# Channel weights from two loads instead of six, first items' channel products moved up, and extra TensorE products between the last weight groups

## The chip, the cores and the metric

The kernel runs on one core of a Trainium2 chip. The metric is device time in microseconds (us) of one execution. Three runs of the kernel before took 184.38, 184.82 and 185.29 us; the median is 184.82.

The core has TensorE (PE in the profile; its weight loads, which overlap products, are PEld), VectorE (DVE), ScalarE (ACT), GpSimd (POOL) and SyncE (SP). [...]

## The reference

A causal convolution with softmaxed taps per head, then a spectral mix of 64 modes, then a channel product with a residual:

```python
def _attn_ref(x, weight):                     # x: 8 x 3264 x 192, weight: 8 x 7
    w = exp(weight - max) / (sum + 1e-09)     # per head, 7 taps
    ...
    out = np.einsum('hk,bskhg->bshg', w, x_unf)

def _moe_ref(x, w_r, w_i, w_ch):              # x is the convolution's result
    X = np.fft.rfft(x, axis=1)
    Xr, Xi = (np.real(X[:, :n_modes]), np.imag(X[:, :n_modes]))
    Yr = np.einsum('bmd,mde->bme', Xr, w_r) - np.einsum('bmd,mde->bme', Xi, w_i)
    Yi = np.einsum('bmd,mde->bme', Xr, w_i) + np.einsum('bmd,mde->bme', Xi, w_r)
    Y[:, :n_modes] = Yr + 1j * Yi
    y = np.fft.irfft(Y, n=S, axis=1)
    u = x + y
    return u + np.maximum(u @ w_ch, 0.0)
```

## The kernel before

Instructions stand in the order in which the program emits them on each engine (a manual schedule); only the waits are added.

**Loads.** x comes in 13 units (`load_unit`, line 136), two transfers each, issued by POOL; units 6 to 12 are issued at lines 240 and 241. Then come six loads of the channel weights `w_ch` (192 x 192): rows 0 to 127 into `wm`, rows 128 to 191 into partitions 64 to 127 of `w1`, rows 128 to 191 into both halves of `wt2`, and rows 64 to 127 and 0 to 63 into the two halves of `wsw`. The right halves of `wm` and `w1` hold an identity. Then come the mode weights, 16 groups of four modes, two transfers of 288 KB each (`load_w`, line 250): eight groups in a row, and each further group when a mix has freed its place. Eight POOL transfers are in flight at most: each issue waits for the one eight places before it.

**Convolution and forward transform.** `conv_pass` multiplies x by band matrices and writes the result back into `xall`, one slot further left (x of the first unit is loaded from slot 1 on, its result starts in slot 0). `dft` multiplies it by a table of cosines and sines; `xtrans` transposes the sums.

**Mix.** The main loop runs over pairs of groups, d = 0 to 7. `mix(g, bank)` (line 400) makes twelve products of 192 columns from the transposed spectrum and the group's weights; `mix_copy` (ACT) takes the result out of PSUM, `mix_trans` transposes it, DVE and ACT copy it into `yet`. In between, `some(n)` takes jobs off the list `tjobs`: `g_bank` and `c_bank`, which transpose the table and the convolved x, eight tiles each, into `ftab` and `ct`. The bank pairs are `zm` (mix) and `ze` (its transposes); four more (`zt4`) serve the jobs.

**The seam.** After the last pair, `zw_mm(b, bank)` multiplies `yet` by `wm` and `w1`, 384 columns each, for the eight batches b; the left 192 columns are the product with the channel weights ("g"), the right 192 the spectrum itself ("y"). `zw_out` copies both, scaled, into `zw`, by DVE or ACT. These eight share the four banks of `zm` and `ze`, so b = 4 to 7 wait for the copies of b = 0 to 3. Items 0 and 1 of the output (`place[0]`, `place[1]`) are done here one product at a time: `c_products(n)` (channel product of the convolved x, six products for each of two halves), `full(n, "g", a)` (adds the spectral share of the channel product), a relu, `full(n, "y", a)` (adds y), and `finish(n)` (DVE adds the convolved x, SP stores).

**The loop.** From line 568 on the other 50 items follow with the same parts (`both`, `relu` on ACT, `finish`) on four bank pairs, two of them laid over the banks of `zm` and `ze`, the first over that of b = 4 and 5.

`wt2` and `wsw` are the right-hand sides for the second and third column block of a "c" product, lines 439 and 440.

Of the kernel before, what the change touches and what calls it, by code (L numbers as in the profile page):

```python
# [9 lines left out]
ALU = mybir.AluOpType  # L10
ACT = mybir.ActivationFunctionType
AX = mybir.AxisListType
F32 = mybir.dt.float32
BF16 = mybir.dt.bfloat16
# [5 lines left out]
def kernel(  # L20
# [9 lines left out]
    nc = tc.nc  # L30
    B, S, D = x.shape
# [5 lines left out]
    P = 128  # L37
# [4 lines left out]
    NT = 2 * NB  # L42
# [8 lines left out]
    units = [(q, b0, n) for q in range(NQ) for b0, n in (UNITS if q else UNITS0)]  # L51
# [3 lines left out]
    def sb(name, shape, dtype):  # L55
        return pool.tile([P] + shape, dtype, tag=name, name=name)
# [5 lines left out]
    xall = sb("xall", [NSLOT, 2, D], BF16)  # L62
# [5 lines left out]
    zw = mixa[:, 0:2 * B * D].rearrange("p (t b d) -> p t b d", t=2, b=B)  # L68
    band = sb("band", [H, 2 * P], BF16)
    wm = sb("wm", [2 * D], BF16)  # L70
    w1 = sb("w1", [2 * D], BF16)
    wt2 = sb("wt2", [D], BF16)
    wsw = sb("wsw", [D], BF16)
    ident = sb("ident", [P], BF16)
    perm = sb("perm", [P], BF16)
    ascale = sb("ascale", [1], F32)
# [40 lines left out]
    def open_psum(side, widths):  # L117

        if side in stacks:
            stacks.pop(side).close()  # L120
        es = ExitStack()
        n = npool[0]
        npool[0] += 1
        p = es.enter_context(tc.tile_pool(name=f"ps{n}", bufs=1, space=PSUM, side=side, reuse_waits="tile"))
        stacks[side] = es
        return [p.tile([P, w, 512], F32, tag=f"z{n}_{i}", name=f"z{n}_{i}") for i, w in enumerate(widths)]
# [9 lines left out]
    def load_unit(q, b0, n):  # L136
        t0 = 2 * b0
        nf = min(2 * n, NF - t0)
        s0 = NT * q + t0 + 1
        for i in range(2):  # L140
            off = ((2 * q + i) * S + P * t0) * D
            src = bass.AP(tensor=x.tensor, offset=x.offset + off, ap=[[D, P], [P * D, nf], [1, D]])
            nc.gpsimd.dma_start(out=xall[:, s0:s0 + nf, i, :], in_=src)  # L143
# [24 lines left out]
    for _ in range(NIDLE):  # L168
        nc.tensor.matmul(ZC[2][:, 0, 0:2 * D], xall[:, 0, 0, 0:P], xall[:, 0, :, :], start=True, stop=True,
                         skip_group_check=True)  # L170
    nc.vector.tensor_scalar(out=cidx[:, 0:PW], in0=cidx[:, 0:PW], scalar1=goff[:, 0:1], scalar2=None, op0=ALU.add)
    for k in range(KK):
        nc.vector.tensor_scalar(out=masks[:, PW * k:PW * (k + 1)], in0=cidx[:, 0:PW],
                                scalar1=float(KK - 1 - k), scalar2=None, op0=ALU.is_equal)
# [16 lines left out]
    for g in range(4):  # L191
        dst, srcv = band[32 * g:32 * g + 32, :, 32 * g:32 * g + PW], pk3[32 * g:32 * g + 32, :, :]
# [39 lines left out]
    for u in units[4:6]:  # L232
# [4 lines left out]
                            fill=1.0, base=0, pattern=[[-1, D]], channel_multiplier=1)  # L237
    nc.gpsimd.affine_select(out=w1[64:P, D:2 * D], in_=w1[64:P, D:2 * D], compare_op=ALU.not_equal,
                            fill=1.0, base=P, pattern=[[-1, D]], channel_multiplier=1)
    for u in units[6:]:  # L240
        load_unit(*u)
    nc.gpsimd.dma_start(out=wm[:, 0:D], in_=moe_w_ch[0:P, :])
    nc.gpsimd.dma_start(out=w1[64:P, 0:D], in_=moe_w_ch[P:D, :])
    for i in range(2):
        nc.gpsimd.dma_start(out=wt2[64 * i:64 * i + 64, :], in_=moe_w_ch[P:D, :])
        nc.gpsimd.dma_start(out=wsw[64 * i:64 * i + 64, :], in_=moe_w_ch[64 - 64 * i:P - 64 * i, :])

    NG = MODES // 4

# [104 lines left out]
    zt4 = open_psum("left", (1, 1, 1, 1))  # L354
    z4 = open_psum("right", (1, 1, 1, 1))
    ze, zm = [z[:, 0, :] for z in z4[0:2]], [z[:, 0, :] for z in z4[2:4]]
    for z in zm:
        nc.vector.memset(z[:, 0:2 * D], 0.0)
    tbank = [0]
# [28 lines left out]
            trans(tp[:, P * k:P * k + P], row[:, P * w:P * w + P])  # L388
        copy(ct[:, k0:k0 + 8, :].rearrange("p t s -> p (t s)"), tp[:, 0:8 * P])

    tjobs = [(g_bank, 8 * k, min(8, NT - 8 * k)) for k in range((NT + 7) // 8)]
    tjobs += [(c_bank, k) for k in range(0, 3 * NT * NQ, 8)]

    def some(n):
        for _ in range(n):
            if tjobs:
                f, *a = tjobs.pop(0)
                f(*a)

    def mix(g, bank):  # L400
        yp = bank[:, D * (g % 2):D * (g % 2) + D]
        for j in range(3):
            for p4 in range(4):
                m = 4 * g + p4
                nc.tensor.matmul(yp[32 * p4:32 * p4 + 2 * B, :], xt[:, j, :, m],  # L405
                                 wts[g][:, p4, j, :], start=(j == 0), stop=(j == 2),
                                 tile_position=(0, 32 * p4), skip_group_check=True)
        if g < NW:
            load_w(g + NW + 3)
        elif g >= NW + 3:  # L410
            load_w(g + NW)

    def mix_copy(d, bank, g0, n):
        nc.scalar.copy(out=ymix[d % 2][:, g0:g0 + n, :],  # L414
                       in_=bank[:, D * g0:D * (g0 + n)].rearrange("p (g d) -> p g d", g=n))

    def mix_trans(d, g0, n):
        et = [z.bitcast(BF16)[:, 0:n * P].rearrange("p (g k) -> p g k", g=n) for z in ze]
        for t in range(2):
            for g in range(n):  # L420
                trans(et[t][:, g, :], ymix[d % 2][:, g0 + g, 64 * t:64 * t + P])
        m0 = 8 * d + 4 * g0
        for t in range(2):
            dst = yet[:, t, :, :].rearrange("p b (c m) -> p c b m", c=2)[:, :, :, m0:m0 + 4 * n]
            srcv = et[t].rearrange("p g (q k) -> p (g q) k", q=4)[:, :, 0:16].rearrange(
                "p m (c b) -> p c b m", c=2)
            if t == 0:
                nc.vector.tensor_copy(out=dst, in_=srcv)
            else:
                nc.scalar.copy(out=dst, in_=srcv)  # L430

    def z_pieces(u, row, which):
        r = slice(64 * row, 64 * row + 64)
        q, t = u
        if which == "c":
            b0, b1 = slice(0, D), slice(D, 2 * D)
            lhs = [ct[r, 3 * (NT * q + t) + w, :] for w in range(3)]
            if row == 0:
                return [(b0, lhs[0], wm[r, 0:D]), (b0, lhs[1], wt2[r, :]), (b1, lhs[2], wsw[r, :])]
            return [(b0, lhs[0], wm[r, 0:D]), (b1, lhs[1], wsw[r, :]), (b1, lhs[2], wt2[r, :])]  # L440
        return [(slice(0, 2 * D), ftab[r, t, :],
                 zw[r, 0 if which == "g" else 1, 2 * q:2 * q + 2, :].rearrange("p b d -> p (b d)"))]

# [27 lines left out]
    def zw_mm(b, bank):  # L471
        nc.tensor.matmul(bank[:, 0:2 * D], yet[:, 0, b, :], wm[:], start=True, stop=False)  # L472
        nc.tensor.matmul(bank[:, 0:2 * D], yet[:, 1, b, :], w1[:], start=False, stop=True)  # L473

    def zw_out(b, bank, on_scalar=None):
        dst = zw[:, :, b, :]
        srcv = bank[:, 0:2 * D].rearrange("p (t d) -> p t d", t=2)
        if on_scalar or (on_scalar is None and b % 2):
            nc.scalar.activation(out=dst, in_=srcv, func=ACT.Copy, scale=ascale[:, 0:1])
        else:  # L480
            nc.vector.tensor_scalar(out=dst, in0=srcv, scalar1=ascale[:, 0:1], scalar2=None, op0=ALU.mult)
# [3 lines left out]
    place = {}  # L485
# [22 lines left out]
    def c_products(n):  # L508
        for first in range(2):
            both(n, first, "c", begin=(first == 0))  # L510

    def full(n, which, a):
        (q, t), _ = duos[n]
        nc.tensor.matmul(place[n][0][a][:, 0:2 * D], ftab[:, t + a, :],  # L514
                         zw[:, 0 if which == "g" else 1, 2 * q:2 * q + 2, :].rearrange("p b d -> p (b d)"),
                         start=False, stop=(which == "y"), skip_group_check=True)
# [2 lines left out]
    while pend:  # L519
        xtrans(pend.pop(0), ze)  # L520
    ND = NG // 2
    for d in range(ND - 1):
        mix(2 * d, zm[d % 2])
        mix(2 * d + 1, zm[d % 2])
        mix_copy(d, zm[d % 2], 0, 2)
        some(4 if d < ND - 2 else 2)
        mix_trans(d, 0, 2)
        some(4 if d < ND - 2 else 99)
    sl = open_psum("left", (1, 1, 2))
    place[0] = ([z[:, 0, :] for z in sl[0:2]], None)  # L530
    place[1] = ([sl[2][:, i, :] for i in range(2)], sl[2])
    d = ND - 1
    mix(NG - 2, zm[1])
    mix_copy(d, zm[1], 0, 1)
    c_products(0)
    mix_trans(d, 0, 1)
    c_products(1)
    mix(NG - 1, zm[0])
    mix_copy(d, zm[0], 1, 1)
    mix_trans(d, 1, 1)  # L540
    zb4 = zm + ze
    for b in range(4):
        zw_mm(b, zb4[b])
    for b in range(4):
        zw_out(b, zb4[b])
    for a in range(2):
        full(0, "g", a)
    b0, b1 = place[0][0]
    nc.vector.tensor_scalar(out=b0[:, 0:2 * D], in0=b0[:, 0:2 * D], scalar1=0.0, scalar2=None, op0=ALU.max)
    nc.scalar.activation(out=b1[:, 0:2 * D], in_=b1[:, 0:2 * D], func=ACT.Relu)  # L550
    for b in range(4, 6):
        zw_mm(b, zb4[b - 4])
    for a in range(2):
        full(0, "y", a)
    for a in range(2):
        full(1, "g", a)
    for b in range(4, 6):
        zw_out(b, zb4[b - 4], True)
    finish(0)
    for b in range(6, 8):  # L560
        zw_mm(b, zb4[b - 4])
    relu(1)
    for b in range(6, 8):
        zw_out(b, zb4[b - 4], False)
    zz = open_psum("right", (2, 2))
    zz = [zz[1], None, zz[0], None]

    for n in range(2, N + 2):
        if n == 3:
            zz[1::2] = open_psum("left", (2, 2))  # L570
        if n < N:
            z = zz[(n - 2) % 4]
# [48 lines left out]
```

## Time and profile before

| | |
|---|---|
| median of three runs | 184.82 us |
| profiled execution, its own time | 183.83 us |
| its span in the profile | 182.1 us |
| TensorE busy | 162.3 us (89%) |
| DVE, ACT, POOL busy | 113.7, 98.4, 51.3 us |
| mean granted TensorE clock | 0.968 |
| loaded by POOL's queue (as written) | 19.64 MB |
| stored by SP's queue | 20.09 MB |

The prediction's sums are made against the profiled execution. A row of the timeline has start and duration in us, engine, line, operation, what is written and read, shapes, the count, and in brackets the engine's idle time before it and what ended it. A row of a stretch has from and to, its length, the busy time of PE, PEld, DVE, ACT and POOL with counts, the granted clock (1.00 is full), the busy share of the DMA engines (packets overlap, so it can pass 1) and GB/s. A row of the chain of waits has start, duration and what it was. "idle before" and releasers are inferred from semaphores.

### The profile page before, as it was taken

What the parts mean: (1) busy time and instruction counts of PE and PEld (TensorE: products, weight loads), DVE (VectorE), ACT (ScalarE), POOL (GpSimd) and SP (SyncE); (2) the same over time, 40 slices, a digit from 0 to 9 for tenths busy, and PEclk for the clock granted to TensorE, in tenths of its full rate; (3) what the DMA queues carried; (4) which work ended last, traced back from release to release, by engine and by line L of the source; (5) the groups of instructions that cost most, each with busy time, mean ns of one, the idle gap of its engine ahead of it and who ended that gap; (6) DMA issues with size and microseconds to landing.
All of it is one profiled execution on the core that took longest, in us unless ns stands there. A gap on an engine that the chain in (4) does not pass through costs nothing.

```text
span 182.1 us, 6281 instructions
## 1 busy us (share of the span) xinstructions
PE 162.3 (89%) x2738; PEld 124.2 (68%) x2738; DVE 113.7 (62%) x173; ACT 98.4 (54%) x138; POOL 51.3 (28%) x82
## 2 busy tenths in 40 slices
PE   7978979999999988999774389999999999999980
PEld 3567969999999967988673135566666666666640
DVE  6679864365455446766581005678777877877782
ACT  6348774344434435766643115566666666666650
POOL 7998844443232944444441000000000000000000
PEclk9999999999999999999999756999999999999998
DMA  4999999999999999999999930468988898888886
GB/s 53 148 188 191 193 191 192 193 191 192 193 192 169 172 205 206 208 205 206 208 205 207 206 59 0 158 238 315 336 303 315 320 315 324 311 327 317 316 320 223
DMA packets 50139, 40.12 MB, mean 220 GB/s; under 512 B 28608, under 2 KB 50112, under 8 KB 50112
## 3 DMA queue, kind: packets, MB, share of 16 engines
q0 software_dynamic: 35808, 19.64, 78.6%
q1 hardware_dynamic: 14304, 20.09, 30.1%
q8 instruction: 21, 0.34, 0.8%
q14 instruction: 6, 0.05, 0.1%
HBM read 39.30 MB, written 20.05 MB: 326 GB/s over the span
## 4 chain that ended last, share of the span: by engine, by line
DMA 48%; PE 39%; POOL 7%; issue 3%; DVE 1%; ACT 1%; POOLq 0%; DVEq 0%
PE z L466 35%; DMA xall<-in_x_dram 25%; DMA arena<-in_moe_w_i_dram 16%; DMA ct<-in_moe_w_i_dram 6%; POOL xall L143 4%; PE z L472 1%; PE z L473 1%; POOL arena L253 1%; PE z L514 1%; PE z L405 1%; POOL xall L231 1%; DVE arena L502 1%; ACT z L490 0%; PE z L375 0%; POOL perm L226 0%
## 5 line engine op out<-in xcount | busy, mean ns | idle before, releaser
L502 DVE TENSOR_TENSOR arena<-z,xall 128x768 f32<-128x768 f32 (+2 forms) x53 | 49.8, 942 | 14.5 <-ACT z L490 13.8
L490 ACT ACTIVATE z<-z 128x768 f32<-128x768 f32 x51 | 40.6, 795 | 22.0 <-PE z L466 22.0
L466 PE MATMUL z<-mixa,ftab 64*128 64x384 bf16 x400 | 49.4, 323 | 0.4 <-ACT z L490 0.3
L272 PE MATMUL z<-xall,band 128*64 128x192 bf16 (+3 forms) x832 | 39.0, 246 | 3.1 <-DMA xall<-in_x_dram 1.2
L466 PEld LDWEIGHTS <-ct 64*128 64x128 bf16 x624 | 24.7, 95 | 22.5 <-PE z L466 15.4
L272 PEld LDWEIGHTS <-band 128*64 128x64 bf16 x832 | 36.6, 110 | 4.8 <-issue 2.6
L281 DVE CAST xall<-z 128x768 bf16<-128x768 f32 (+3 forms) x26 | 24.8, 956 | 22.3 <-PE z L272 20.6
L466 PE MATMUL z<-wt,ct 64*128 64x192 bf16 x208 | 35.0, 247 | 0.0
L466 PE MATMUL z<-wsw,ct 64*128 64x192 bf16 x208 | 34.2, 247 | 0.0
L279 ACT CAST xall<-z 128x768 bf16<-128x768 f32 (+3 forms) x26 | 20.7, 798 | 20.5 <-PE z L272 20.4
L143 POOL DMA_DIRECT2D xall<-in_x_dram x26 | 23.6, 912 | 13.3 <-DMA xall<-in_x_dram 12.4
L466 PE MATMUL z<-wm,ct 64*128 64x192 bf16 x208 | 26.5, 251 | 0.2
L367 DVE COPY ct<-z 128x1024 bf16<-128x1024 bf16 x26 | 17.1, 686 | 8.3 <-PE z L375 5.7
L290 PE MATMUL z<-xall,ftab 128*64 128x384 bf16 (+1 forms) x208 | 21.0, 326 | 0.7 <-ACT xall L279 0.7
L375 PE MATMUL z<-ident,xall 128*128 128x128 bf16 x312 | 19.3, 219 | 0.0
L466 PEld LDWEIGHTS <-ftab 64*128 64x128 bf16 x400 | 18.1, 94 | 1.4 <-PE z L466 0.8
L375 PEld LDWEIGHTS <-xall 128*128 128x128 bf16 x312 | 17.7, 98 | 0.7
L365 ACT COPY ct<-z 128x1024 bf16<-128x1024 bf16 x13 | 13.2, 1012 | 4.4 <-PE z L375 4.4
L290 PEld LDWEIGHTS <-ftab 128*64 128x64 bf16 (+1 forms) x208 | 13.5, 110 | 2.3 <-DVE xall L281 0.5
L405 PE MATMUL z<-arena,mixa 128*16 128x192 bf16 x156 | 6.0, 272 | 7.4 <-DMA arena<-in_moe_w_i_dram 6.7
L405 PEld LDWEIGHTS <-mixa 128*16 128x16 bf16 x192 | 4.2, 127 | 10.4 <-DMA arena<-in_moe_w_i_dram 7.7
L414 ACT CAST ymix<-z 128x384 bf16<-128x384 f32 (+1 forms) x9 | 4.0, 444 | 12.8 <-PE z L405 12.8
(86 smaller groups left out, 117.7 us busy)
## 6 DMA issues: line engine op xcount, KB each, us to landing
out_dram<-arena SPq DMA_DIRECT2D x47, 384.0 KB, 3.1
xall<-in_x_dram POOLq DMA_DIRECT2D x14, 384.0 KB, 15.7
arena<-in_moe_w_r_dram POOLq DMA_DIRECT2D x13, 288.0 KB, 10.8
arena<-in_moe_w_i_dram POOLq DMA_DIRECT2D x13, 288.0 KB, 11.0
xall<-in_x_dram POOLq DMA_DIRECT2D x6, 432.0 KB, 16.7
out_dram<-arena SPq DMA_DIRECT2D x4, 288.0 KB, 3.7
ct<-in_moe_w_r_dram POOLq DMA_DIRECT2D x3, 288.0 KB, 11.5
ct<-in_moe_w_i_dram POOLq DMA_DIRECT2D x3, 288.0 KB, 11.5
```

Of the source, the lines that this page charges most:

```text
L143: nc.gpsimd.dma_start(out=xall[:, s0:s0 + nf, i, :], in_=src)
L272: nc.tensor.matmul(o, lhs, xall[:, r0:r0 + 2 * n - 1:2, :, dsl], start=(main and a == 0), stop=not main, tile_position=(0, 64 * half), ski ...
L279: nc.scalar.copy(out=dst, in_=srcv)
L281: nc.vector.tensor_copy(out=dst, in_=srcv)
L290: nc.tensor.matmul(xp[r, :], ftab[0:k, t, r], xall[0:k, NT * q + t, :, :], start=(t == 0), stop=(t == NT - 1), tile_position=(0, 64 * hh), ...
L365: nc.scalar.copy(out=out, in_=in_)
L367: nc.vector.tensor_copy(out=out, in_=in_)
L375: nc.tensor.matmul(o, in_, ident[:], start=True, stop=True, is_transpose=True)
L405: nc.tensor.matmul(yp[32 * p4:32 * p4 + 2 * B, :], xt[:, j, :, m], wts[g][:, p4, j, :], start=(j == 0), stop=(j == 2), tile_position=(0, 3 ...
L466: mm = nc.tensor.matmul(banks[bank][:, cols], l, r, start=(begin and k == 0), stop=(end and k == len(lst) - 1), skip_group_check=True)
L490: nc.scalar.activation(out=z, in_=z, func=ACT.Relu)
L502: nc.vector.tensor_tensor(out=o[0:pn, :, a:a + w, :].rearrange("p i a d -> p a i d"), in0=zin, in1=xall[0:pn, s + a:s + a + w, :, :], op=A ...
```

## The change

Four loads go: both of `wt2` and both of `wsw`. The loads of `wm` and `w1` are issued between those of x, after unit 7 and unit 8. A new job `w_bank`, fifth in `tjobs` after the four `g_bank`, makes what was loaded: two TensorE products with the signed permutation `perm`, a DVE copy with a factor of -1 into the upper partitions of `wsw` (now 384 columns) and an ACT copy into the lower ones; the third reader takes `w1` directly.

`c_products(0)` and `(1)` are moved from the last pair of groups to the place before pair d = 6. Around the mixes of groups 12 to 15 new products `warm(bank, n)` are put: they multiply slot 0 of `xall` by itself into a bank that is not in use, 12, 3 and 5 times in pair 6, and 2 and 13 times in pair 7; nothing reads what they write.

In the seam, the copies of b = 0 and 1 are cut into halves, "g" first; the order of `full`, `zw_mm`, `zw_out` and `finish` is changed, and `zw_mm(7)` is put behind the copy of b = 3.

```diff
-    wt2 = sb("wt2", [D], BF16)
-    wsw = sb("wsw", [D], BF16)
+    wsw = sb("wsw", [2 * D], BF16)
...
-    for u in units[6:]:
+    for k, u in enumerate(units[6:]):
         load_unit(*u)
-    nc.gpsimd.dma_start(out=wm[:, 0:D], in_=moe_w_ch[0:P, :])
-    nc.gpsimd.dma_start(out=w1[64:P, 0:D], in_=moe_w_ch[P:D, :])
-    for i in range(2):
-        nc.gpsimd.dma_start(out=wt2[64 * i:64 * i + 64, :], in_=moe_w_ch[P:D, :])
-        nc.gpsimd.dma_start(out=wsw[64 * i:64 * i + 64, :], in_=moe_w_ch[64 - 64 * i:P - 64 * i, :])
+        if k == 1:
+            nc.gpsimd.dma_start(out=wm[:, 0:D], in_=moe_w_ch[0:P, :])
+        if k == 2:
+            nc.gpsimd.dma_start(out=w1[64:P, 0:D], in_=moe_w_ch[P:D, :])
...
+    def w_bank():
+
+        z = zt4[tbank[0] % 4][:, 0, 0:2 * D]
+        tbank[0] += 1
+        nc.tensor.matmul(z[:, 0:D], perm[:], wm[:, 0:D], start=True, stop=True, skip_group_check=True)
+        nc.tensor.matmul(z[:, D:2 * D], perm[:], w1[:, 0:D], start=True, stop=True, skip_group_check=True)
+        nc.vector.tensor_scalar(out=wsw[0:64, :], in0=z[0:64, :], scalar1=-1.0, scalar2=None, op0=ALU.mult)
+        nc.scalar.copy(out=wsw[64:P, 0:D], in_=z[64:P, 0:D])
+
-    tjobs = [(g_bank, 8 * k, min(8, NT - 8 * k)) for k in range((NT + 7) // 8)]
+    tjobs = [(g_bank, 8 * k, min(8, NT - 8 * k)) for k in range((NT + 7) // 8)] + [(w_bank,)]
...
-                return [(b0, lhs[0], wm[r, 0:D]), (b0, lhs[1], wt2[r, :]), (b1, lhs[2], wsw[r, :])]
-            return [(b0, lhs[0], wm[r, 0:D]), (b1, lhs[1], wsw[r, :]), (b1, lhs[2], wt2[r, :])]
+                return [(b0, lhs[0], wm[r, 0:D]), (b0, lhs[1], wsw[r, D:2 * D]), (b1, lhs[2], wsw[r, 0:D])]
+            return [(b0, lhs[0], wm[r, 0:D]), (b1, lhs[1], wsw[r, 0:D]), (b1, lhs[2], w1[r, 0:D])]
...
-    def zw_out(b, bank, on_scalar=None):
-        dst = zw[:, :, b, :]
-        srcv = bank[:, 0:2 * D].rearrange("p (t d) -> p t d", t=2)
-        if on_scalar or (on_scalar is None and b % 2):
+    def zw_out(b, bank, on_scalar, t=None):
+        ts = slice(0, 2) if t is None else slice(t, t + 1)
+        dst = zw[:, ts, b, :]
+        srcv = bank[:, 0:2 * D].rearrange("p (t d) -> p t d", t=2)[:, ts, :]
+        if on_scalar:
...
-    for d in range(ND - 1):
+
+    def warm(bank, n):
+
+        for _ in range(n):
+            nc.tensor.matmul(bank[:, 0:2 * D], xall[:, 0, 0, 0:P], xall[:, 0, :, :], start=True, stop=True,
+                             skip_group_check=True)
+
+    for d in range(ND - 2):
         mix(2 * d, zm[d % 2])
         mix(2 * d + 1, zm[d % 2])
         mix_copy(d, zm[d % 2], 0, 2)
-        some(4 if d < ND - 2 else 2)
+        some(4)
         mix_trans(d, 0, 2)
-        some(4 if d < ND - 2 else 99)
+        some(4 if d < ND - 3 else 99)
     sl = open_psum("left", (1, 1, 2))
...
+    c_products(0)
+    c_products(1)
+    d = ND - 2
+    mix(2 * d, zm[0])
+    warm(zm[1], 12)
+    mix(2 * d + 1, zm[0])
+    mix_copy(d, zm[0], 0, 2)
+    warm(zm[1], 3)
+    mix_trans(d, 0, 2)
+    warm(zm[1], 5)
     d = ND - 1
     mix(NG - 2, zm[1])
     mix_copy(d, zm[1], 0, 1)
-    c_products(0)
+    warm(zm[0], 2)
     mix_trans(d, 0, 1)
-    c_products(1)
+    warm(zm[0], 13)
     mix(NG - 1, zm[0])
     mix_copy(d, zm[0], 1, 1)
     mix_trans(d, 1, 1)
     zb4 = zm + ze
-    for b in range(4):
-        zw_mm(b, zb4[b])
-    for b in range(4):
-        zw_out(b, zb4[b])
+    zw_mm(0, zb4[0])
+    zw_mm(1, zb4[1])
+    for t in range(2):
+        zw_out(0, zb4[0], False, t)
+        zw_out(1, zb4[1], True, t)
+    zw_mm(2, zb4[2])
+    zw_mm(3, zb4[3])
+    b0, b1 = place[0][0]
+    full(0, "g", 0)
+    nc.vector.tensor_scalar(out=b0[:, 0:2 * D], in0=b0[:, 0:2 * D], scalar1=0.0, scalar2=None, op0=ALU.max)
+    full(0, "g", 1)
+    nc.scalar.activation(out=b1[:, 0:2 * D], in_=b1[:, 0:2 * D], func=ACT.Relu)
     for a in range(2):
-        full(0, "g", a)
-    b0, b1 = place[0][0]
-    nc.vector.tensor_scalar(out=b0[:, 0:2 * D], in0=b0[:, 0:2 * D], scalar1=0.0, scalar2=None, op0=ALU.max)
-    nc.scalar.activation(out=b1[:, 0:2 * D], in_=b1[:, 0:2 * D], func=ACT.Relu)
-    for b in range(4, 6):
-        zw_mm(b, zb4[b - 4])
+        full(1, "g", a)
+    zw_mm(4, zb4[0])
+    zw_mm(5, zb4[1])
     for a in range(2):
         full(0, "y", a)
-    for a in range(2):
-        full(1, "g", a)
-    for b in range(4, 6):
-        zw_out(b, zb4[b - 4], True)
+    zw_out(2, zb4[2], True)
     finish(0)
-    for b in range(6, 8):
-        zw_mm(b, zb4[b - 4])
     relu(1)
-    for b in range(6, 8):
-        zw_out(b, zb4[b - 4], False)
+    zw_mm(6, zb4[2])
+    for b in range(3, 7):
+        zw_out(b, zb4[b % 4], b % 4 < 2)
+    zw_mm(7, zb4[3])
+    zw_out(7, zb4[3], False)
```

## The prediction

> **What bounds the kernel now.** The page comes first: its span and its strips of the granted clock and of the DMA share.
>
> ```profile
> span 182.1 us, 6281 instructions
> PEclk9999999999999999999999756999999999999998
> DMA  4999999999999999999999930468988898888886
> ```
>
> A slice is 4.55 us. The transfers fill the first 23 slices, up to about 105 us, and pause before the output starts. The clock is down in slices 23 to 25, at that seam. Next the chain of waits, read from its end backwards:
>
> ```profile
> 104.19 0.69 PE z L405 x10
> ...
> 109.50 0.50 PE z L472
> ...
> 116.53 59.28 PE z L466 x968
> ```
>
> Ahead of 104.19 the chain is a line of DMA landings; that product is the mix of group 14, released by its weights. From 116.53 TensorE runs 59.28 us without a pause. So three stretches add up: the load stream to 104.19, the seam to the loop's entry, the output loop. The change edits the first two and leaves the loop's work as it is.
>
> **The load stream.** The timeline of POOL and the table of DMA issues show the loads that go away:
>
> ```profile
> 54.27 0.52 POOL L246 DMA_DIRECT2D wsw<-in_moe_w_ch_dram  x1 [1.59 <-DMA xall<-in_x_dram]
> 56.84 0.63 POOL L253 DMA_DIRECT2D arena<-in_moe_w_r_dram  x1 [2.05 <-ACT xs L294]
> 58.85 0.62 POOL L253 DMA_DIRECT2D arena<-in_moe_w_i_dram  x1 [1.38 <-DMA xall<-in_x_dram]
> ...
> wt<-in_moe_w_ch_dram POOLq DMA_DIRECT2D x2, 24.0 KB, 9.3
> wsw<-in_moe_w_ch_dram POOLq DMA_DIRECT2D x2, 24.0 KB, 7.2
> ```
>
> Each issue waits until the load eight places ahead of it has landed (the program's waits name eight lanes in turn), so eight loads are in flight. At 54.27 the last of six channel-weight loads is issued; now six of the eight lanes hold such small loads, and the large mode weights wait for a lane: one issue at 56.84, the next at 58.85. Busy share and GB/s in stretches of 2 us (last two columns) show the price:
>
> ```profile
> 54.00:56.00 2.00, 2.00 (x44) 1.92 (x42) 0.65 (x2) 0.80 (x1) 0.52 (x1) 1.00 1.59 194
> 56.00:58.00 2.00, 2.00 (x52) 1.96 (x50) 1.00 (x2) 1.28 (x2) 0.63 (x1) 1.00 1.52 177
> 58.00:60.00 2.00, 2.00 (x44) 1.90 (x41) 1.44 (x3) 0.48 (x1) 1.15 (x2) 1.00 1.19 157
> 60.00:62.00 2.00, 2.00 (x43) 1.96 (x39) 1.17 (x2) 0.80 (x1) 1.99 (x5) 1.00 1.03 137
> 62.00:64.00 2.00, 2.00 (x37) 1.88 (x34) 0.60 (x1) 0.96 (x1) 1.82 (x4) 1.00 1.19 198
> 64.00:66.00 2.00, 1.28 (x23) 0.98 (x20) 1.75 (x3) 0.96 (x1) 1.18 (x2) 1.00 1.21 205
> ```
>
> Against 194 before, some 200 where x and weights mix, and 205 after, the dip lost 2 us x (17/194 + 43/200 + 68/205 + 7/205) = 1.34 us. The four removed loads wrote 4 x 24.6 kB = 98 kB, 0.49 us at 200 GB/s. After the change the two remaining small loads sit between x loads, so whole x loads fill the lanes at the seam from x to weights. That takes away what made the dip: 0.49 + 1.34 = 1.83 us. The bounds are 0.49 (bytes alone, the dip stays) and 1.83; I take the upper one, because the dip begins where the lanes are full of small loads and ends when they are not. The moved loads delay x units 8 to 12 by 74 kB, 0.37 us, at no cost as long as the convolutions have that slack: the last x load has landed by 58.85 (its successor's issue) and TensorE was busy all of each stretch up to 64 us. Losing that cover costs at most the 0.37.
>
> [...]
>
> **What makes the copies instead.** The added job of two 192-column products, one DVE and one ACT copy falls into the stretch after 70 us, where TensorE is ahead of the weights. I count nothing; without cover its products would cost about 0.2 us at the pitch below, and the copies about 0.6.
>
> **TensorE ahead of group 14.** Here the order changes most.
>
> ```profile
> 95.63 0.46 PE L405 MATMUL z<-arena,mixa 128*16 128x192 bf16 x12 [0.97 <-DMA arena<-in_moe_w_i_dram]
> 96.02 1.07 PE L375 MATMUL z<-ident,xall 128*128 128x128 bf16 x16
> ...
> 101.37 0.46 PE L405 MATMUL z<-arena,mixa 128*16 128x192 bf16 x12 [2.45 <-DMA arena<-in_moe_w_i_dram]
> 101.93 0.48 ACT L414 CAST ymix<-z 128x384 bf16<-128x384 f32 x1 [4.08 <-PE z L405]
> 102.46 0.34 PEld L375 LDWEIGHTS <-ymix 128*128 128x128 bf16 x4 [0.83 <-ACT ymix L414]
> ...
> 112.48 0.33 PE L472 MATMUL z<-wm,yet 128*128 128x384 bf16 x1
> 112.64 0.33 PE L473 MATMUL z<-w,yet 128*128 128x384 bf16 x1
> ```
>
> The last two rows give the pitch of a 384-column product at full clock, 0.16 us; a warming product has that shape. In the old trace's time, group 11 lands at 95.63 - 1.83 = 93.8. Then come 0.4 us of mix, 24 transposes (1.6), four more, about 0.7 until the last copy frees its bank (an estimate: half as long again as the 0.48 of the ACT copy above), and the 24 c products of two items (192 columns, half of 0.16 each, and two row halves partly side by side: 1.2): mix 12 starts near 97.9. Twelve warming products (1.9) and the mix bring mix 13 to 100.2, where its weights have landed (101.37 - 1.83 = 99.5). From mix to transposes is 102.46 - 101.37 = 1.1, then five warming products, 0.8: TensorE is ready at 102.3, and group 14 lands at 104.19 - 1.83 = 102.36. So it just fits; if the copies are 1 us late, 1 us goes through to the end.
>
> **The clock.** Stretches before and at the fall, and at the start of the kernel, where the old code multiplies zeros:
>
> ```profile
> L169 PE MATMUL z<-xall x40: 326/326/524, 1.3 to 10.2; 128*128 128x384 bf16 x40
> ...
> 5.00:6.00 1.00, 1.00 (x4) 0.44 (x3) 0.38 (x2) 1.00 (x1) 1.00 (x3) 1.00 1.20 118
> 7.00:8.00 1.00, 1.00 (x8) 0.60 (x7) 0.93 (x3) 0.00 (x0) 1.00 (x2) 1.00 1.48 172
> ...
> 101.00:102.00 1.00, 0.46 (x12) 0.26 (x12) 0.00 (x0) 0.07 (x1) 0.00 (x0) 1.00 1.20 204
> 102.00:103.00 1.00, 0.54 (x4) 0.34 (x4) 0.11 (x1) 0.41 (x1) 0.00 (x0) 0.52 1.21 205
> ```
>
> Line 169 goes from four products a microsecond to eight after some 5 us of nothing but such products: they do raise the clock. The clock fell at 102, after a 2.45 us gap and little work. The new order leaves TensorE gaps under 1 us from group 12 on, so I take the full clock. One thing differs from the description: the slot that the warming products read was zero at line 169, but the convolution of the first item writes its result there, so they multiply data. I give that no price.
>
> [...]
>
> **From group 14 to the loop.**
>
> ```profile
> 104.98 0.32 ACT L414 CAST ymix<-z 128x192 bf16<-128x192 f32 x1 [1.61 <-PE z L405]
> ...
> 105.00:106.00 1.00, 0.94 (x12) 0.38 (x8) 0.00 (x0) 0.30 (x1) 0.00 (x0) 0.50 0.93 158
> 106.00:107.00 1.00, 1.00 (x12) 0.41 (x8) 0.23 (x1) 0.21 (x1) 0.00 (x0) 0.50 0.27 44
> ...
> 107.78 0.69 PE L405 MATMUL z<-arena,mixa 128*16 128x192 bf16 x12
> ...
> 110.43 0.62 DVE L481 TENSOR_SCALAR mixa<-z,ascale 128x384 bf16<-128x384 f32 x1 [0.99 <-PE z L473]
> 110.99 0.58 ACT L479 ACTIVATE mixa<-z,ascale 128x384 bf16<-128x384 f32 x1 [1.46 <-PE z L473]
> 112.52 0.57 DVE L549 TENSOR_SCALAR z<-z 128x384 f32<-128x384 f32 x1 [0.27 <-PE z L514]
> 112.75 0.48 ACT L550 ACTIVATE z<-z 128x384 f32<-128x384 f32 x1
> 113.50 1.02 DVE L502 TENSOR_TENSOR arena<-z,xall 128x384 f32<-128x384 f32 x2 [0.41 <-PE z L514]
> 114.08 0.82 ACT L490 ACTIVATE z<-z 128x768 f32<-128x768 f32 x1
> 114.53 0.26 PE L466 MATMUL z<-wm,ct 64*128 64x192 bf16 x2
> ```
>
> Old: mix 14 at 104.19, mix 15 at 107.78 (3.59 later), channel products at 109.50 (+1.72), loop at 114.53 (+5.03): 10.34 us, nearly all at half clock. Group 15 had landed by about 106.6 (44 KB moved after 106); mix 15 stood behind the c products.
>
> New, at full clock. Mix 14 to its copy 0.56 (from 101.37 to 101.93), copy 0.32, transposes 0.15, then thirteen warming products, 13 x 0.163 = 2.12: mix 15 starts 3.15 after mix 14. Its weights land 2.4 after, so the warming products hold it up by 0.7. Mix 15 to channel products: 1.72 less what the clock saves up to the copy (0.79 from 104.19 to 104.98, against 0.56), 1.5.
>
> From there, counted from the first channel product: half copies on DVE from 0.6 and on ACT from 0.9, some 0.36 and 0.42 each (a little over half of 0.62 and 0.58); the first "g" product at 1.4, the relu on DVE 1.8 to 2.4, its "y" product at 2.7. DVE then runs the item's two additions (1.02) to 4.1 and the copy of b = 3 to 4.7. Channel product 7 waits for that copy and stands ahead of the loop in TensorE's queue, so the loop enters at 5.1. ACT (relu, b = 2, relu of item 1 with 0.82, b = 4 and 5) is done at 4.9. So this part, though at full clock, is as long as before: DVE and ACT take over from TensorE. Bounds: 4.8, ACT's own work without a gap (0.9 + 2 x 0.42 + 0.48 + 3 x 0.58 + 0.82), and 6.1, if each of some five hand-overs is 0.2 late.
>
> Sum: 3.15 + 1.5 + 5.1 = 9.75 against 10.34, so 0.59; with the stream 1.83 + 0.59 = 2.42 us. The profiled execution took 183.83 us (1.73 around its span); that gives 181.4. The median of the runs before is 184.82, 0.99 above it; by the same 2.42, 182.4 us, which I forecast.
>
> **The rivals.**
>
> **The dip stays**, as a matter of the change from x to weights: only 0.49 + 0.59 = 1.08 come off, 183.7 us. For it: the lowest stretch, 137 GB/s, comes after x has landed. Against: POOL's late issues explain that too. Chance 0.17.
>
> **The seam is longer**: TensorE late at group 14, or DVE's queue at the loop's entry, costs 1 us: 183.4 us. For it: 0.1 us of margin. Chance 0.13.
>
> **The clock doesn't hold** (the slower side): the warming products don't count enough, and it falls before mix 13. Then a warming product costs 0.32. Mix 12 at 97.9, with 0.6 and 12 x 0.32 mix 13 at 102.3; 1.3 + 0.5 + 5 x 0.32 mix 14 at 105.7; 1.35 + 13 x 0.32 mix 15 at 111.2; channel products at 112.9 instead of 109.50: 3.4 us late, 188.2 us. It decides once the clock stays low over the thirteen: these alone cost 2.1 more, nearly all the gain. Against: line 169. Chance 0.07.
>
> **How the numbers follow.** The forecast has 0.63. Within 0.5% (0.92 us), about what a measurement of this kernel can tell from no change, lie a few of the first two rivals' cases, where both meet or the dip's share is smaller still: 0.11. Faster 0.81, slower 0.08 (the third rival and a little). The range goes from 181.2 (entry at 4.8, mix 15 released by its weights, and 0.2 for the runs' spread) to 184.2 (the dip stays and half of the second rival).
>
> **What would show it.** Right: no stretch under 190 GB/s between 54 and 64 us; the mix of group 14 near 102.4 with clock 1.00 from there on; thirteen products end after group 15 has landed; some 5 us from the first channel product to the loop, with product 7 waiting for DVE; a loop of 59 us as before. Wrong: a dip of the same depth after the last x load, a half clock in any stretch after 95 us, or mix 14 waiting for TensorE and not for its load.

## The result, and the profile after

The kernel after takes 182.57 us (median of 7 runs, 181.82 to 183.39) against 184.82 before (7 runs, 184.25 to 185.54): ratio 0.9887, interval 0.9856 to 0.9919, 2.25 us less. The forecast was 182.4.

The profiled execution of before (183.83) was faster than all its seven runs and that of after (183.06) is 0.5 above its median, so this pair of traces differs by 0.77 us only; further executions of both follow below. Ratios leave out runs more than 1.5% above the fastest of their kernel, which in zeros, six_early and old_seam_warm10 drops 16 of the 23 runs of before (median 185.93, fastest 182.80), so there the medians stand beside the ratio.

The page after, its span and the strips of clock and DMA share:

```profile
span 181.2 us, 6354 instructions
PEclk9999999999999999999999999999999999999998
DMA  4999999999999999999999910468898888888886
```

The clock no longer falls; the pause of the DMA strip is still there. The stretches of 2 us where the dip was (last two columns: DMA share, GB/s):

```profile
56.00:58.00 2.00, 2.00 (x52) 1.94 (x49) 1.00 (x2) 1.28 (x2) 0.32 (x2) 1.00 1.56 193
58.00:60.00 2.00, 2.00 (x45) 1.92 (x41) 1.44 (x3) 0.48 (x1) 0.43 (x1) 1.00 1.27 205
60.00:62.00 2.00, 2.00 (x43) 1.96 (x39) 1.17 (x2) 0.80 (x1) 0.99 (x2) 1.00 1.22 212
62.00:64.00 2.00, 2.00 (x37) 1.88 (x34) 0.56 (x1) 0.96 (x1) 0.84 (x2) 1.00 1.21 203
```

The dip is gone: 193 to 212 GB/s where there were 177, 157, 137 and 198. The chain of waits after (start, duration, what):

```profile
92.76 11.16 DMA arena<-in_moe_w_i_dram
103.92 0.04 issue
103.97 0.46 PE z L412 x11
...
105.19 2.11 PE z L534 x13
107.31 0.42 PE z L412 x12
...
108.67 0.34 PE z L479
...
112.60 0.62 DVE mixa L489
113.22 0.04 issue
113.27 0.32 PE z L479
...
115.69 59.28 PE z L473 x968
```

Line 412 is the mix, 534 a warming product, 479 the channel product, 473 the loop. Mix 14 still starts when its load lands, at 103.97: 0.22 us sooner than in the first trace of before, not 1.83. The stretch from there to the loop's entry at 113.68 (the row is below) is 9.71 us against 10.34, and the loop is the same 59.28. So in this pair the seam gave 0.63 as forecast, and the load stream hardly anything, although its dip is gone: mix 14 near 102.4, one of the prediction's signs, did not come. Why is the question for the experiments.

A trace has sixteen landing times for each of these loads, its parts: those of group 14's second load run from 102.76 to 104.14 in the first trace of before and from 100.24 to 103.92 in that of after. Here are the first and the last of them, the start of mix 14, which comes right behind, and the time from it to the loop, for all profiles (us; the lower five have the six loads of before):

| kernel | first part | last part | apart | mix 14 | mix 14 to loop |
|---|---|---|---|---|---|
| after | 100.24 | 103.92 | 3.68 | 103.97 | 9.71 |
| after_again | 99.72 | 103.41 | 3.69 | 103.45 | 9.72 |
| loads_only | 100.24 | 103.61 | 3.37 | 103.66 | 10.89 |
| no_warm | 100.59 | 104.50 | 3.91 | 104.54 | 11.27 |
| old_seam | 100.33 | 104.78 | 4.44 | 104.82 | 8.56 |
| two_late | 100.55 | 104.16 | 3.62 | 104.21 | 9.71 |
| reorder_warm10 | 100.42 | 105.12 | 4.70 | 105.16 | 8.16 |
| zeros | 100.32 | 103.40 | 3.08 | 103.44 | 9.72 |
| old_seam_warm10 | 100.02 | 103.15 | 3.14 | 103.20 | 8.19 |
| before | 102.76 | 104.14 | 1.39 | 104.19 | 10.34 |
| before_again | 104.00 | 105.37 | 1.37 | 105.42 | 10.46 |
| before_third | 103.83 | 105.09 | 1.26 | 105.13 | 10.65 |
| seam_only | 104.64 | 106.17 | 1.52 | 106.21 | 9.72 |
| six_early | 100.59 | 103.94 | 3.36 | 103.99 | 10.42 |

Each row is one execution. In all fourteen, mix 14 starts 0.04 to 0.05 us after the last part. The nine kernels with two small loads have a mean last part of 104.01, the four with a dip (all of the lower five but six_early) 105.19: 1.18 us, though the two groups overlap (103.15 to 105.12 against 104.14 to 106.17). Their mean first parts are 100.27 and 103.81: 3.54 us. The mean of all sixteen parts lies between: 101.82 against 104.38, 2.56 us; in the first pair alone it went from 103.48 to 101.71, 1.77 us.

The same times show where the parts draw together. In the loads that land just ahead of the dip they are 1.9 (before), 2.9 (before_again), 2.8 (before_third) and 3.8 us (seam_only) apart; in those that land right behind it, at 64 to 68 us, 0.5 to 1.1. Without a dip they stay as they are there: 2.6 us apart ahead and 2.6 behind in the kernel after.

### The profile page after: what moved, and what is told of

Same layout as the page of the kernel before. It is cut to its first block, busy times and chain, and to the rows that moved or that the text cites. A ratio compares the mean times of both kernels' runs of the same rounds, so it can differ in the third digit from the quotient of the medians.

```text
span 181.2 us, 6354 instructions
## 1 busy us (share of the span) xinstructions
PE 165.0 (91%) x2775; PEld 126.4 (70%) x2775; DVE 114.2 (63%) x175; ACT 98.9 (55%) x140; POOL 49.5 (27%) x78
## 4 chain that ended last, share of the span: by engine, by line
PE 54%; DMA 33%; POOL 6%; issue 3%; DVE 1%; ACT 1%; POOLq 0%; DVEq 0%
PE z L473 34%; DMA arena<-in_moe_w_i_dram 20%; PE z L270 10%; DMA ct<-in_moe_w_i_dram 6%; DMA xall<-in_x_dram 6%; PE z L288 5%; POOL xall L142 4%; PE z L534 1%; PE z L479 1%; DVE arena L510 1%; PE z L522 1%; POOL xall L230 1%; PE z L480 1%; PE z L412 0%; ACT xall L277 0%
## 5 line engine op out<-in xcount | busy, mean ns | idle before, releaser
L270 PE MATMUL z<-xall,band 128*64 128x192 bf16 (+3 forms) x832 | 39.7, 246 | 3.1 <-ACT band L193 1.5
L270 PEld LDWEIGHTS <-band 128*64 128x64 bf16 x832 | 37.3, 110 | 4.9 <-issue 2.3
L473 PE MATMUL z<-wsw,ct 64*128 64x192 bf16 x312 | 33.7, 243 | 0.0
L473 PE MATMUL z<-w,ct 64*128 64x192 bf16 x104 | 25.2, 243 | 0.0
L288 PE MATMUL z<-xall,ftab 128*64 128x384 bf16 (+1 forms) x208 | 22.0, 326 | 0.7 <-ACT xall L277 0.7
L288 PEld LDWEIGHTS <-ftab 128*64 128x64 bf16 (+1 forms) x208 | 14.4, 110 | 2.4 <-issue 0.7
L251 POOL DMA_DIRECT2D arena<-in_moe_w_r_dram x13 | 8.0, 612 | 14.3 <-PE z L373 4.5
L251 POOL DMA_DIRECT2D arena<-in_moe_w_i_dram x13 | 7.9, 611 | 12.5 <-DMA xall<-in_x_dram 5.5
```

Of the source, the lines that this page charges most:

```text
L251: nc.gpsimd.dma_start(out=wts[g][64 * half:64 * half + 64, :, :, :], in_=src[4 * g:4 * g + 4, :, :].rearrange("m (p j) e -> p m j e", j=3))
L270: nc.tensor.matmul(o, lhs, xall[:, r0:r0 + 2 * n - 1:2, :, dsl], start=(main and a == 0), stop=not main, tile_position=(0, 64 * half), ski ...
L288: nc.tensor.matmul(xp[r, :], ftab[0:k, t, r], xall[0:k, NT * q + t, :, :], start=(t == 0), stop=(t == NT - 1), tile_position=(0, 64 * hh), ...
L473: mm = nc.tensor.matmul(banks[bank][:, cols], l, r, start=(begin and k == 0), stop=(end and k == len(lst) - 1), skip_group_check=True)
```

## Experiments on the load stream

**before_again** and **before_third**: the kernel before, unchanged, profiled.

> The kernel before, profiled once more. Its profiled execution took 183.83 us, 1 us under the median of its runs. If that execution was a lucky one of the load stream, group 14's mix starts here near 105.2 and not at 104.19, with seam and loop as long as before; if the loop or the seam varies, the mix starts at 104.2 and they differ.

Mix 14 at 105.42, to the loop 10.46, loop 59.28: it is the load stream that varies, by 1.2 us. Its dip in the same stretches is deeper than in the first trace:

```profile
56.00:58.00 2.00, 2.00 (x52) 2.00 (x49) 1.00 (x2) 1.28 (x2) 0.24 (x1) 1.00 1.49 171
58.00:60.00 2.00, 2.00 (x44) 1.99 (x40) 1.44 (x3) 0.48 (x1) 0.65 (x2) 1.00 0.86 90
60.00:62.00 2.00, 2.00 (x43) 2.00 (x40) 1.17 (x2) 0.80 (x1) 2.00 (x4) 1.00 1.03 152
62.00:64.00 2.00, 2.00 (x36) 1.99 (x34) 0.82 (x1) 0.96 (x1) 2.00 (x5) 1.00 1.13 182
```

Those rows are of before_third, whose expectation was:

> The kernel before, profiled a third time, since the load stream differs from one execution to the next. If the parts of a load run apart only where the stream doesn't pause, the sixteen parts of the last load land within 1.6 us here again (1.4 and 1.3 in the two profiles so far, 3 to 5 where the dip is gone), the first of them after 105.5 and the last near 108, and mix 14 starts at 105 within 0.8. If a spread over 2.5 us shows up here too, the pause has nothing to do with it.

Its sixteen parts land 1.3 us apart, the first of the last load at 106.66, the last at 107.94, mix 14 at 105.13: as expected. By the reckoning of the prediction this dip cost 2 x (23/194 + 110/200 + 53/205 + 23/205) = 2.08 us, not 1.34. Reckoned like this the dips of the four kernels that have one cost 2.05 us on average, with the bytes 2.54: what the mean of the sixteen parts gained (2.56).

**loads_only**: the loads and `w_bank` of the change, with the old pairs and the old seam.

```diff
...
-    for i in range(2):
-        nc.gpsimd.dma_start(out=wt2[64 * i:64 * i + 64, :], in_=moe_w_ch[P:D, :])
-        nc.gpsimd.dma_start(out=wsw[64 * i:64 * i + 64, :], in_=moe_w_ch[64 - 64 * i:P - 64 * i, :])
+        if k == 1:
+            nc.gpsimd.dma_start(out=wm[:, 0:D], in_=moe_w_ch[0:P, :])
+        if k == 2:
+            nc.gpsimd.dma_start(out=w1[64:P, 0:D], in_=moe_w_ch[P:D, :])
...
+    tjobs = [(g_bank, 8 * k, min(8, NT - 8 * k)) for k in range((NT + 7) // 8)] + [(w_bank,)]
```

> The kernel before with the change's loads alone: two channel-weight loads between those of x, the copies made by TensorE; the mix pairs, the c products and the seam as before, no warming products. The prediction's theory: the dip between 56 and 64 us is gone, and the whole 1.83 us come off (ratio about 0.990). The rival, from the traces so far: the landing of a load is set by the slowest of its sixteen parts, which lag further behind without the dip, and 0.2 us come off (ratio 0.999); the spread of the sixteen parts of the last load is then over 3 us.

184.47 against 186.45 us, ratio 0.9898 (0.9849 to 0.9947): 2.0 us, near the prediction's 1.83. The interval, 1.0 to 2.8 us, shuts out the rival's 0.2. But the rival's sign is there too: the last load's parts are 3.4 us apart, and mix 14 starts 1.2 us before the mean of before's three profiles (104.91), 0.5 before the first of them. Neither theory is right alone: the gain is real, but what releases the mix is the slowest part (103.61, the mix starts at 103.66). Whether it is worth 1.2 or 1.83 the timed runs can't tell.

**six_early**: the six loads of before, in pairs behind units 6, 7 and 8.

```diff
...
+    for k, u in enumerate(units[6:]):
         load_unit(*u)
...
+        if k < 3:
+            w_load(2 * k)
+            w_load(2 * k + 1)
```

> The kernel before with its six small loads issued in pairs behind units 6, 7 and 8, between those of x. Same bytes as before, old mix pairs and seam. If six lanes full of small loads at the change from x to weights make the dip, the dip is gone and 1 to 1.5 us come off (ratio 0.992 to 0.995, all of the loads' gain but the 0.5 of the bytes). If the number of loads as such costs, wherever they stand, the ratio is 1.000.

```profile
56.00:58.00 2.00, 2.00 (x52) 1.95 (x49) 1.00 (x2) 1.30 (x3) 0.14 (x1) 1.00 1.58 194
58.00:60.00 2.00, 2.00 (x44) 1.86 (x41) 1.44 (x3) 0.49 (x2) 0.61 (x1) 1.00 1.33 204
60.00:62.00 2.00, 2.00 (x44) 1.95 (x40) 1.17 (x2) 0.80 (x1) 0.99 (x2) 1.00 1.22 211
```

With the same six loads the dip is gone (194 to 211 GB/s against 177, 157 and 137 in the first trace of before), so lanes full of small loads at the change from x to weights make it. The time does not follow: 185.35 against 185.93, ratio 1.0014 (0.9965 to 1.0062), which is the sign of the rival, that the number of loads costs wherever they stand. By the medians it is 0.6 us, still less than the 1 to 1.5 expected. The profile can't settle it, as its execution (183.66) was the fastest of the 12. So it is shown that these lanes make the dip, and not shown that taking away the dip alone gives more than some 0.6 us.

**two_late**: the kernel after with its two loads behind all of x.

```diff
...
-        if k == 1:
-            nc.gpsimd.dma_start(out=wm[:, 0:D], in_=moe_w_ch[0:P, :])
-        if k == 2:
-            nc.gpsimd.dma_start(out=w1[64:P, 0:D], in_=moe_w_ch[P:D, :])
+    nc.gpsimd.dma_start(out=wm[:, 0:D], in_=moe_w_ch[0:P, :])
+    nc.gpsimd.dma_start(out=w1[64:P, 0:D], in_=moe_w_ch[P:D, :])
```

> The kernel after with its two small loads issued behind all x loads, where the six were. Same bytes as after. If the dip comes from the number of lanes that small loads hold, two of eight leave a small dip (under 0.4 us; ratio within 0.002 of after). If the place alone makes it, the dip is as deep as before and 1.3 to 2 us are lost.

183.28 us, ratio 0.9864 (0.9822 to 0.9906), the very ratio of after beside it; its lowest stretch between 54 and 64 us is 190 GB/s. Two small loads make no dip at either place (193 at the lowest in after), and six make one only where they stand together behind x (94 at the lowest in seam_only, 194 in six_early); moving the two was not needed.

## Experiments on the clock and the seam

**seam_only**: the kernel after with the six loads of before at their old place.

> The kernel after with the six loads of before: the moved c products, the warming products and the new order of the seam alone. The prediction's theory: 0.59 us come off (ratio 0.997), with the dip of before and group 14's mix when its load lands. Rival: the seam is worth the whole measured 2.2 us (ratio 0.988), since the clock is up.

184.65 against 186.45, ratio 0.9922 (0.9891 to 0.9953): 1.5 us by the ratio, 0.9 to 2.0 by its interval, so more than 0.59. Its own seam takes 9.72, like after's. What differs is the seam of the old kernels, which is 10.34 only in the first trace: 10.46 and 10.65 in the others, and 10.89 in loads_only. That makes 0.83 us on average; what is left of the 1.5 these profiles don't explain. Stretches of loads_only, granted clock third from the end:

```profile
111.00:112.00 1.00, 1.00 (x5) 0.46 (x4) 0.62 (x1) 0.30 (x2) 0.00 (x0) 0.50 0.00 0
112.00:113.00 1.00, 1.00 (x6) 0.46 (x4) 0.57 (x1) 0.79 (x2) 0.00 (x0) 0.56 0.00 0
113.00:114.00 1.00, 1.00 (x8) 0.61 (x7) 0.48 (x2) 0.98 (x2) 0.00 (x0) 1.00 0.00 0
```

Its channel products begin at 108.95, and the clock is back only near 112.9, 3.9 us later (2.8 in the first trace of before, 3.0 in before_again): nearly the whole seam runs at half clock. In the first trace of before half clock lasts 10.24 us, from 102.03 to 112.28, and in no_warm 10.2, from 102.32 to 112.56 by the clock of its rows; in loads_only it lasts 12.1 us at least, as mix 13, at 100.82, already takes 0.69 us, where mix 12 took 0.46 at 97.50. So it begins and ends at another time in each of these executions. Its end isn't tied to the seam, and the old seam costs more in some executions than in the first trace.

**no_warm**: the kernel after with `range(0)` in `warm`.

> The kernel after without its 35 warming products. If these hold the clock, it falls to half between 100 and 104 us, mix 14 to the channel products and the seam's products take about twice as long, and 1 to 3 us are lost against the kernel after (ratio to before 0.995 to 1.005). If the moved c products and the denser order hold it alone, the clock stays at 1.00 and the kernel is 0.3 us faster than after, as mix 15 no longer waits for thirteen products.

```profile
101.00:102.00 1.00, 0.28 (x12) 0.26 (x12) 0.00 (x0) 0.00 (x0) 0.00 (x0) 1.00 1.22 206
102.00:103.00 1.00, 0.36 (x14) 0.18 (x3) 0.00 (x0) 0.48 (x1) 0.00 (x0) 0.66 1.22 209
103.00:104.00 1.00, 0.43 (x4) 0.17 (x2) 0.29 (x1) 0.27 (x1) 0.00 (x0) 0.50 0.81 137
```

The clock falls at 102.3. In these rows TensorE is busy 28 to 43%, and the gap that ends at 101.72, ahead of the fall, is 1.64 us long. Mix 14 to the loop takes 11.27 us, 1.55 more than with the products. 185.01 us, ratio 0.9911 (0.9873 to 0.9950), against after's 0.9887 and 0.9864: intervals that overlap, so the loss of some 0.5 us in time is not settled, while the clock is plain: its mean is 0.955 to 0.968 in all nine runs, and 0.984 to 0.998 in the thirteen of after and after_again. The extra products do hold it.

**zeros**: the warming products read a tile of zeros.

```diff
...
-            nc.tensor.matmul(bank[:, 0:2 * D], xall[:, 0, 0, 0:P], xall[:, 0, :, :], start=True, stop=True,
+            nc.tensor.matmul(bank[:, 0:2 * D], zero[:, 0:P], zero[:], start=True, stop=True,
```

> The kernel after with warming products that read a tile of zeros in place of the first convolved slot. If what is multiplied matters to the clock or the time, the clock falls somewhere after 100 us or the ratio differs from after's 0.986 by over 0.004; if only the instruction counts, clock 1.00 and the same ratio within the interval.

```profile
core 0: 180.7 us, clock 0.992
```

182.93 against 185.93 (medians: 0.984; the ratio is 0.9939, 0.9881 to 0.9998), mean clock 0.992 like after's 0.996 and 0.994, mix 14 to the loop 9.72. By the letter of the expectation the ratio, 0.008 from after's, would say that it matters; the medians are 0.002 away. By the profile what is multiplied makes no difference.

**after_again**: the kernel after, for its ratio on this chip.

> The kernel after, unchanged, for its ratio beside the others of this chip and a second profile. The prediction's theory: group 14's mix starts when its load lands, 2 us before that of the kernel before on average; 3.2 us from there to mix 15, 1.4 to the channel products, 5.0 to the loop. Rival from the first trace (slowest of sixteen parts): the mix starts near 104 again although the fastest part of the last load is in by 103.

183.20 against 185.62, ratio 0.9864 (0.9829 to 0.9898). Mix 14 at 103.45, 1.5 us before the mean of before's three and between the two signs, then 3.28 to mix 15, 1.43 to the channel products, 5.01 to the loop.

**old_seam**: the kernel after with before's order of copies, relu and products behind mix 15.

```diff
-    for t in range(2):
-        zw_out(0, zb4[0], False, t)
-        zw_out(1, zb4[1], True, t)
...
+    for b in range(4):
+        zw_out(b, zb4[b], b % 2 == 1)
...
-    zw_mm(7, zb4[3])
-    zw_out(7, zb4[3], False)
+    for b in range(6, 8):
+        zw_mm(b, zb4[b - 4])
+    relu(1)
+    for b in range(6, 8):
+        zw_out(b, zb4[b - 4], False)
```

> The kernel after with the seam's old order behind mix 15 (all copies whole, old order of full, zw_mm, zw_out and finish), at full clock. The prediction says the new order takes 5.1 us from the first channel product to the loop, as the old one did at half clock. If the new order gains by itself, the old one at full clock takes longer than 5.0 and this kernel is slower than after; if the old order at full clock is as fast or faster (4 to 4.5 us by its rows, since its copies don't stand behind the additions), the change's reordering gave nothing.

The timeline of the kernel after, DVE's end of the seam and TensorE's wait for it:

```profile
111.67 1.02 DVE L510 TENSOR_TENSOR arena<-z,xall 128x384 f32<-128x384 f32 x2 [0.73 <-PE z L522]
112.60 1.80 DVE L489 TENSOR_SCALAR mixa<-z,ascale 128x384 bf16<-128x384 f32 x3
113.27 0.32 PE L479 MATMUL z<-wm,yet 128*128 128x384 bf16 x1 [1.15 <-DVE mixa L489]
...
113.68 0.26 PE L473 MATMUL z<-wm,ct 64*128 64x192 bf16 x2
```

And old_seam, first channel product, DVE's copies of b = 0 and 2, the additions, the loop:

```profile
109.52 0.34 PE L479 MATMUL z<-wm,yet 128*128 128x384 bf16 x1 [0.26 <-DVE yet L435]
...
110.13 1.20 DVE L489 TENSOR_SCALAR mixa<-z,ascale 128x384 bf16<-128x384 f32 x2 [0.67 <-PE z L480]
...
112.35 1.02 DVE L510 TENSOR_TENSOR arena<-z,xall 128x384 f32<-128x384 f32 x2 [0.41 <-PE z L522]
...
112.64 0.33 PE L479 MATMUL z<-wm,yet 128*128 128x384 bf16 x1
```

In the new order TensorE stands 1.15 us in front of product 7, which needs the copy of b = 3, which DVE makes after the additions. In the old order that copy is long made: the loop enters at 113.38, 3.86 us after the first channel product, not 5.01. The ratio is 0.9829 (0.9785 to 0.9874) against 0.9864 beside it, better by a third of a per cent, inside the intervals. So the new order gives nothing; in the profiles its wait for product 7 costs the 1.15 us by which its seam is longer (9.71 against 8.56), in the timed runs 0.4 of it shows.

**reorder_warm10** and **old_seam_warm10**: two ways to take that wait away, both with ten products before mix 15.

```diff
-    warm(zm[0], 13)
+    warm(zm[0], 10)
...
     zw_out(2, zb4[2], True)
+    zw_out(3, zb4[3], False)
+    zw_out(4, zb4[0], True)
+    zw_out(5, zb4[1], True)
     finish(0)
     relu(1)
     zw_mm(6, zb4[2])
-    for b in range(3, 7):
-        zw_out(b, zb4[b % 4], b % 4 < 2)
     zw_mm(7, zb4[3])
+    zw_out(6, zb4[2], False)
     zw_out(7, zb4[3], False)
```

> The kernel after with the copy of b = 3 put ahead of the item's additions on DVE, b = 4 and 5 ahead of item 1's relu on ACT, channel product 7 behind product 6 at once, and ten warming products in place of thirteen before mix 15. If DVE's and ACT's order sets the loop's entry, it comes some 4 us after the first channel product in place of 5.0, and mix 15 comes up to 0.5 sooner unless its load holds it: 1 to 1.5 us under after (ratio to before 0.980 to 0.984). If TensorE sets it, nothing changes but the 0.5.

181.44 against 185.62, ratio 0.9781 (0.9741 to 0.9820): 1.8 us under after on the same chip, and the two intervals don't meet.

```profile
111.67 0.61 DVE L489 TENSOR_SCALAR mixa<-z,ascale 128x384 bf16<-128x384 f32 x1
111.75 1.52 ACT L487 ACTIVATE mixa<-z,ascale 128x384 bf16<-128x384 f32 x3
...
112.50 1.02 DVE L510 TENSOR_TENSOR arena<-z,xall 128x384 f32<-128x384 f32 x2 [0.22 <-PE z L522]
...
113.32 0.26 PE L473 MATMUL z<-wm,ct 64*128 64x192 bf16 x2
```

The copy of b = 3 now lies in the gap of DVE before the additions, ACT makes its three copies in a row, and the loop enters 3.81 us after the first channel product at 109.51. Of the 1.56 us by which this seam is shorter than after's, 1.20 lie there; 0.36 lie ahead of mix 15, where three products fewer stand.

> The kernel after with the seam's old order and ten warming products in place of thirteen before mix 15. If the old order at full clock is as good as the new order of reorder_warm10 (3.9 and 3.8 us from the first channel product to the loop in their profiles), both have the same ratio, 0.978 to 0.983; if the earlier copies of that kernel count beyond the loop's entry, this one is 0.5 us slower.

181.33 against 185.93 (medians: 0.975; ratio 0.9838, 0.9746 to 0.9930). Mix 14 to the loop is 8.19 us, the other's 8.16: the two orders are equal within what was measured.

## Why the prediction was right

**The dip**: right. It is gone with two loads (193 to 212 GB/s), six_early (194 to 211) shows that lanes full of small loads made it, and two_late (190 at the lowest) that two such loads are too few.

**What it is worth, 1.83 us**: the term of the sum that was mis-sized. Mix 14 moved by 0.22 in the pair of traces that the sum was made for, and by 1.18 in the means. The step that failed reckoned the lost time from the mean GB/s of all sixteen parts. For the mean of the parts that sum was right: in the pair it moved by 1.77 us. But mix 14 starts 0.04 to 0.05 us after the last part of its load, in all fourteen traces. Over the pause of the stream the parts drew together (from 1.9 us to 1.0 in before, from 2.9 to 0.6 in before_again); without it they stayed apart, at group 14 by 3.1 to 4.7 us in place of 1.3 to 1.5.

Why some parts lag was not tried, and the trace doesn't name what carried a part, but it gives a hint. Between 67 and 104 us of the traces of before and after the spread grew by over 0.25 us from one load to the next three times: from 1.01 to 1.57 and from 1.32 to 2.03 in before, from 2.81 to 3.69 in after. Each time it was in a load that landed 2.0 to 2.7 us after a packet of 16 KB in the queue for instructions had started (at 69.36 and 76.97, and at 89.83; they took 0.94 to 0.97 us). But the other seven such packets of that stretch bring no such step, and no run changed them, so this is a coincidence seen, not a cause shown.

**TensorE ahead of group 14**: right, and as close as said. In the trace after it has 0.1 us to spare when the load lands. Both times are 1.5 us later than forecast, by about as much as group 11, with which TensorE's work towards it begins: its mix starts at 95.43 and not at 93.8.

**The clock**: right; 1.00 from 95 to 179.6 us, and no_warm, where it fell at 102.3, shows that the products hold it. The length of the gaps, by which the prediction argued, didn't decide it here: in no_warm the clock fell behind gaps of 1.68 and 1.64 us at most, while in the trace of after a gap of 1.87 us, ahead of group 11's mix, passed without a fall.

**3.15, 1.5 and 5.1 us**: measured 3.26, 1.44 and 5.01. Group 15's landing was put too early: 107.03 in the first trace by its last part, not 106.6, so the thirteen products held mix 15 back by 0.4 after the change (107.23 against 106.83), not 0.7. That DVE's order would make the seam at full clock as long as the old one at half was right, and old_seam shows what it means: the new order is itself the cost.

**0.59 us for the seam**: 0.63 in the profiled pair; against the mean of the five old seams at half clock (10.55) it is 0.83, since the clock doesn't come back at the same point of the seam each time (2.8, 3.0 and 3.9 us after the first channel product).

So the total was right with a stream term too large (0.22 in the pair of traces, 1.18 on average) and a seam term a little too small; 1.18 + 0.83 = 2.01, and 2.25 was measured. That the forecast (2.42) came within 0.2 us of it is partly luck: the two errors go opposite ways, and 0.24 us of the 2.25 these means don't explain. How the 2.25 divides stays open: timed alone the loads gave 2.0 us (1.0 to 2.8) and the rest of the change 1.5 (0.9 to 2.0), 3.5 together, and these intervals are too wide to say whether the two gains overlap. Of the rivals, the dip that stays fell by the trace, the longer seam by 9.71 against 9.75, the clock that falls by its strip.

## What to carry to other kernels

Price a pause in a load stream by the part of a load that lands last, not by the mean throughput: between the first two traces the mean of the parts of group 14's load moved by 1.77 us, its last part and the mix behind it by 0.22. Filler products kept TensorE's clock here through the waits for loads (0.984 to 0.998 on average, 0.955 to 0.968 without them), but count them so that they end before the load lands: thirteen held mix 15 back by 0.4 us. When a stall at half clock goes, look again at the order of work behind it: the order that was free before can become the next wait, and here a few copies put ahead of additions and a relu shortened the seam's last part from 5.0 to 3.8 us.

## What the runs showed of the hardware

The sixteen parts of a load of 288 KB ran 3.1 to 4.7 us apart at group 14 in the ten executions without a dip, another amount in each; with one, 0.5 to 1.1 us right behind it and 1.3 to 1.5 at group 14.

In the first trace of before the granted clock was 1.00 from 6.46 to 102.03 us, 0.50 to 112.28 and 1.00 again to 180.54; in that of after it was 1.00 from 5.54 to 179.62. It fell behind 3.4 us (98.60 to 102.00) in which TensorE was busy 23% of the time in before, and at 102.32 in no_warm, behind two us of 8 and 28%; in after 2 us of 28% (94 to 96) passed at 1.00. It came back at 112.28 in before, 112.56 in no_warm, 112.88 in loads_only and 113.76 in before_again, and in all four TensorE had been busy all the time from 111 on. With nothing but transposes on TensorE, from 75 to 78 us in before and busy all the time, the clock stood at 1.00. Over the execution it was 0.996 and 0.994 with warming products on data (after, after_again) and 0.992 with products on zeros.
